# One written order for the transfers of two queues, a written buffer layout, and a new order of all steps, in clustered attention followed by an MLP

## The chip, the cores and the metric

The kernel runs on one core of a Trainium2 chip. The core has TensorE for matrix products (PE in the profile), VectorE (DVE), ScalarE (ACT), GpSimd (POOL) and a sync engine (SP); the last does no arithmetic here and only issues transfers. ACT issues transfers too, between its own computations. The metric is the device time of one execution in microseconds (us).

## The reference: what is computed

Four batches of eight heads, 768 positions, head size 64, all in float32. Each query and each key is put into one of 16 clusters of its head, the one whose normalised centroid it is nearest to. Attention runs only between positions of the same cluster. The heads' outputs, laid side by side, are the input x (4 x 768 x 512) of a second block: a mix over positions by two thin matrices U and V of rank 32, then an MLP of width 2,048 with a residual.

```python
mask = q_assign[:, :, :, None] == k_assign[:, :, None, :]
scores = np.where(mask, scale * np.matmul(q, k.transpose(0, 1, 3, 2)), -1e9)
attn = softmax(scores)                     # over the keys
x = heads_side_by_side(np.matmul(attn, v))
u = x + (x.transpose(0, 2, 1) @ U @ V).transpose(0, 2, 1)
out = u + np.maximum(u @ w_ch1, 0.0) @ w_ch2
```

The second block's weights come as float64 and are turned into float32 on the chip.

## The kernel before, in words

**The work and its order.** `list_work` lists all the work as steps: a call of a small function, or one piece of such a call. `sequence` (line 93) is a list of 4,334 step numbers, the order in which the steps are written out. There is no other schedule: `keep_order` (line 311) ties each instruction to the one written before it on the same engine, so that each engine's own order is the written one. `kept` (line 42) says, with one character for each use, which of a few buffers of a kind each use gets (the probabilities `pr` have 11, the score tiles `st` 2, the general tiles `w` of the matrix results 4, and so on); `place` (line 343) reads it.

**Attention.** It is done in 16 pairs of heads; i is the number of the pair (4 to a batch). Queries and keys are loaded (`load`, R), split into a high and a low part that matmuls take at a faster rate (`split_hi`, `split_lo`), and laid into `arena` (three sets, used in turn) by transfers within the chip: `place_keys_hi`, `place_keys_lo`, `place_queries`, `place_clusters`, and `place_ones`, which fills a row with ones. The one-hot cluster numbers are further rows, scaled so that two positions of different clusters get a score of almost minus infinity. `rowmax` makes the scores once to take each query's maximum on DVE; `rowmax_place` turns the 12 columns of maxima with a matmul, negates them on ACT (mT) and issues a transfer from ACT's queue that lays them into the arena as the row that meets the ones. `scores` makes the scores again, transposed and with the maximum taken off (L781, and L783 which reads the ones and the maxima); ACT takes the exponential (pr, L787); `values` multiplies by v (L805); `weights` adds up the probabilities on POOL, in a few cases on DVE (T, L797). `sums`, `sums_T`, `copy_values` (L811) and `normalise` finish a pair into x (`xt`).

**The mix and the MLP.** `mix_u`, `mix_sum`, `mix_v` do the rank-32 mix; the result goes to memory (u_scr). `fetch_blocks` (line 992) reads it back in eight transfers of 32-row blocks for one half of a batch, and `turn_blocks` transposes the blocks on DVE (L1004). `split_u` makes the high part on ACT (L1016) and the low part on DVE (L1018). The two weight products of the MLP are done by a scheme of seven products of half-size blocks instead of eight: `product` (L1068 to L1070, combined on DVE in L1078 or copied by ACT in L1082), `relu` (L1110 low half on DVE, L1112 high half on ACT), `gemm2` (L1269 to L1271, the second product of batches 0 and 1), and for batches 2 and 3 `product2` (L1215 to L1217), fed by `split_h` (ACT L1142, DVE L1140) and ended by `combine2` and `output`, which sends blocks out in four transfers a time (L1259).

**The weights.** `convert` loads float64 words, joins them to float32 (`join_late`) and stores them to memory (w_scr); `fetch_w` reads one back (w2f, rw). `split_w` and `split_w2` make high and low parts (ACT L1043 and L1052). `sums_w2` reads w_scr with ACT's queue (late_g, turned), adds blocks on POOL and stores the sums from ACT's queue; `keep_w2` and `keep_sums` store from ACT's queue too. `stage_w` reads weights back for batches 2 and 3 (rw, sums_w), `split_staged` splits them (L1164 on ACT, L1162 on DVE or POOL), `load_w2` reads parts for `product2`.

**Transfers.** There are 767: 645 on SP's queue and 122 on ACT's. All those of attention are SP's but one kind, the maxima of `rowmax_place`. A transfer signals its end on a semaphore, of which there are few, so that many transfers share one in turn. In the kernel before only the order on each queue is tied to the written one; how transfers of the two queues follow each other in the turns is left to the framework.

**Buffers.** Tiles of attention lie in pools (`sb` on the left, `late` on the right) that are closed when the MLP opens its own (`open_mlp`, `open_late`); a tile of the MLP that lies over an attention tile waits for that tile's last use. Where a tile lies within its pool follows from when it is first used.

Of the kernel before, what the change touches and what calls it, by code (L numbers as in the profile page):

```python
# [10 lines left out]
F32 = mybir.dt.float32  # L11
F32R = mybir.dt.float32r
# [11 lines left out]
DM = H * D  # L24
# [17 lines left out]
kept = {  # L42
    "R":
        "0101010101010101010110101110100110",
    "rw_g":
        "010110101010101010101010101010101010101010101010101010101010101101001011010101010",
    "rw":
        "0110101010101010101010101010101010010101010110101010",
    "rw_t":
        "0100101010101010110011010101010010101010101010101011001011010011001101001011010",  # L50
    "w":
        "01202301323210210301202012012033022112032101320231303123123212310212310230213013203112010323012013201203213121"
        "02301302301230231011323023101021031212301302321030213023121021023130201320132013201321203103123013021013032102"
        "13021321032012031021012310310231320203121032032102210321030232310312013302320123101232310320120121023310210320"
        "12301320103213010320132102313021301322132013210321020130121320132012301231023132010212013030123023103213032102"
        "31023012313210301230212103312012320123013201023021310321032123021130210203230123012312001302130210303012021013"
        "22012301301032103132012101021302210",
    "pr":
        "0123456789a0123456789a0123456789a0123456789a0123456789a0123465789a132546078a91234560789a1234560789a1234560789a"
        "1234560789a1234560789a12345607891a243560789a12346507891a234506879a123456071892435a60",  # L60
# [5 lines left out]
        "0101010101010101",  # L66
    "mT":
        "01010101010101010",
    "vt":
        "0120121021210210",  # L70
    "st":
        "01010010101010101010101010101010101010101010101010101010101010101010101011001011001010101010101010101010101010"
        "1010101010101010101010101010100110100110101010101010101010101010010110101010010101100101",
# [3 lines left out]
        "01200120120120120120120120120120",  # L77
    "rv":
        "0101010101010101",
    "hh":  # L80
# [3 lines left out]
    "v":  # L84
        "01010101010100110011010101101100111000110101000101010010110101011010001010101010110010101010101010101101010101"
        "100101011011010101100",
    "y":
        "01234540215350342152301540342513124035204153105204123543204130545210352410352134053021352401345202314010532543"
        "51503210421234015343204532015024351023405",
# [1410 lines left out]
```

## Time and profile before

| | |
|---|---|
| time of the runs, us | 967.59, 970.29, 973.48 (median 970.29) |
| the profiled execution, us | 971.04 |
| its span from first to last instruction, us | 969.2 |
| mean granted clock of TensorE | 0.987 |
| busy us: TensorE, its weight loads, DVE, ACT, POOL | 934.8, 747.3, 767.0, 461.9, 642.1 |
| busy share of TensorE | 96% |

In the profile's rows a line such as L783 is a line of the kernel; names are those of tiles, as out<-in. "A <- B C" in a list of waits says that A's engine sat idle until B's instruction that writes C ended; three numbers behind it are the sum in us, how many times, and the longest. SPq and ACTq are the engines' queues of transfers. The granted clock is a share of TensorE's full speed. The chain of waits goes back from the last instruction, at each step to what released it.

### The profile page before, as it was taken

The page shows a single profiled execution, that of the slowest core. Times are in us where ns is not written, and L with a number is a line of the kernel's source. Part 1 is how long each engine was busy: PE and PEld are TensorE (multiplying, and loading weights), DVE is VectorE, ACT ScalarE, POOL GpSimd, SP SyncE. Part 2 cuts the span into 40 slices and gives each one's busy share as a digit, 9 for nine tenths or more (in the row PEclk, how much of TensorE's full clock was granted, in tenths as well). Part 3 has the DMA queues.
Part 4 walks back from the last instruction along what each step waited for, and adds up shares of the span by engine and source line. Part 5 has one row for each costly group of instructions (what it writes and reads, how often), then busy time and mean ns, then how long its engine had stood idle before and what let it go on. Part 6 is the DMA issues. An engine that isn't in the chain of part 4 may idle for free.

```text
span 969.2 us, 14666 instructions
## 1 busy us (share of the span) xinstructions
PE 934.8 (96%) x5098; PEld 747.3 (77%) x5098; DVE 767.0 (79%) x1251; ACT 461.9 (48%) x680; POOL 642.1 (66%) x433
## 2 busy tenths in 40 slices
PE   7999999999999999988899999999899999989997
PEld 5666666666666656644788888889789999989997
DVE  5989988878888877766787768877678988778775
ACT  6545555555555554643433434343434554255440
POOL 6388676788688869985889976875453663137420
PEclk8999999999999999989899999999999999999999
DMA  7666547555756668612548886579768788876686
GB/s 189 177 148 178 143 128 232 141 145 140 212 154 177 179 130 197 74 48 87 196 152 297 313 312 193 160 254 294 209 231 185 166 280 259 227 174 119 231 264 160
DMA packets 169646, 183.13 MB, mean 189 GB/s; under 512 B 110427, under 2 KB 119253, under 8 KB 168549
## 3 DMA queue, kind: packets, MB, share of 16 engines
q1 hardware_dynamic: 136672, 156.21, 58.2%
q10 hardware_dynamic: 32900, 25.99, 8.5%
q8 instruction: 40, 0.66, 0.3%
q14 instruction: 34, 0.27, 0.1%
HBM read 112.72 MB, written 41.42 MB: 159 GB/s over the span
## 4 chain that ended last, share of the span: by engine, by line
PE 82%; DVE 7%; DMA 5%; issue 2%; ACT 2%; POOL 2%; SPq 0%; ACTq 0%; DVEq 0%; POOLq 0%
PE o_ps L805 13%; PE ps_max L750 7%; PE ps_h L1068 7%; PE ps_h L1070 7%; PE ps_h L1069 7%; PE st L781 7%; PE st L783 6%; PE z L1216 4%; PE z L1215 4%; PE z L1217 4%; PE y L1271 4%; PE y L1270 3%; PE y L1269 3%; DVE m L755 2%; PE ps_sum L820 1%
## 5 line engine op out<-in xcount | busy, mean ns | idle before, releaser
L797 POOL TENSOR_TENSOR T<-T,pr 128x768 f32<-128x768 f32 x120 | 223.6, 1867 | 46.2 <-DVE T L797 22.9
L755 DVE TENSOR_REDUCE m<-ps_max 128x1 f32<-128x384 f32 x372 | 189.2, 549 | 45.2 <-PE ps_max L750 43.0
L787 ACT ACTIVATE pr<-st 128x768 f32<-128x768 f32 x186 | 147.2, 811 | 79.9 <-PE st L783 73.3
L805 PE MATMUL o_ps<-pr,vt 128*64 128x384 f32 x768 | 138.8, 499 | 0.0
L1068 PE MATMUL ps_h<-arena,combos 128*128 128x384 f32 x352 | 120.8, 343 | 8.2 <-ACT rw_g L1082 3.5
L1070 PE MATMUL ps_h<-arena,combos 128*128 128x384 f32 x352 | 119.3, 339 | 0.0
L1069 PE MATMUL ps_h<-arena,combos 128*128 128x384 f32 x352 | 119.2, 339 | 0.0
L750 PE MATMUL ps_max<-arena 128*128 128x384 f32 x372 | 113.0, 368 | 2.4 <-DVE m L755 1.6
L805 PEld LDWEIGHTS o_ps<-pr,vt 128*64 128x64 f32 x768 | 50.3, 138 | 65.2 <-issue 60.0
L781 PE MATMUL st<-arena 128*128 128x384 f32 x372 | 100.1, 350 | 0.4 <-ACT pr L787 0.4
L783 PE MATMUL st<-arena 97*128 97x384 f32 x372 | 96.3, 340 | 2.9 <-DMA arena<-ones 2.4
L750 PEld LDWEIGHTS ps_max<-arena 128*128 128x128 f32 x372 | 65.8, 188 | 42.0 <-DVE m L755 18.1
L797 POOL TENSOR_TENSOR T<-pr 128x768 f32<-128x768 f32 x30 | 56.1, 1870 | 53.8 <-ACT pr L787 49.5
L781 PEld LDWEIGHTS st<-arena 128*128 128x128 f32 x372 | 65.0, 189 | 18.4 <-issue 9.0
L1068 PEld LDWEIGHTS ps_h<-arena,combos 128*128 128x128 f32 x352 | 66.9, 190 | 15.3 <-DVE c L1078 5.3
L1271 PE MATMUL y<-w,hl 128*128 128x512 f32 x192 | 76.3, 397 | 1.3 <-DVE hl L1110 1.3
L1270 PE MATMUL y<-w,hh 128*128 128x512 f32 x192 | 76.0, 396 | 0.0
L1269 PE MATMUL y<-w,hh 128*128 128x512 f32 x192 | 75.2, 392 | 0.0
L1162 POOL TENSOR_TENSOR combos<-rw,combos 128x1024 fp32r<-128x1024 f32 x10 | 24.0, 2402 | 74.3 <-ACT combos L1164 74.3
L783 PEld LDWEIGHTS st<-arena 97*128 97x128 f32 x372 | 68.4, 190 | 3.5 <-issue 2.7
L1069 PEld LDWEIGHTS ps_h<-arena,combos 128*128 128x128 f32 x352 | 67.0, 190 | 2.3 <-issue 0.2
L1070 PEld LDWEIGHTS ps_h<-arena,combos 128*128 128x128 f32 x352 | 66.9, 190 | 0.0
(213 smaller groups left out, 2078.8 us busy)
## 6 DMA issues: line engine op xcount, KB each, us to landing
combos<-w_scr SPq DMA_DIRECT2D x112, 256.0 KB
R<-in_qk SPq DMA_DIRECT2D x32, 384.0 KB
arena<-arena SPq DMA_DIRECT2D x64, 192.0 KB
arena<-arena SPq DMA_DIRECT2D x31, 384.0 KB
late_rw<-in_w SPq DMA_DIRECT2D x20, 512.0 KB
u<-u_scr SPq DMA_DIRECT2D x96, 96.0 KB
rw<-w_scr SPq DMA_DIRECT2D x15, 512.0 KB
vt<-in_v SPq DMA_DIRECT2D x16, 384.0 KB
```

The lines of the kernel that those rows point to most:

```text
L750: nc.tensor.matmul(ps[:, 0:HS], x1[:, 0, g // 2, g % 2, t * P:(t + 1) * P], x1[:, 1, h, g % 2, :], start=True, stop=True)
L755: nc.vector.reduce_max(live["m2", i][:, h, u:u + 1], ps[:, 0:HS], axis=AX.X)
L781: nc.tensor.matmul(st[:, j, 0:HS], x1[:, 1, hk, j, ks], x1[:, 0, h, j, :], start=True, stop=False)
L783: nc.tensor.matmul(st[:, j, 0:HS], x2[0:97, 1, hk, j, ks], x2[0:97, 0, h, j, :], start=False, stop=True)
L787: nc.scalar.activation(pr, st[:, :, 0:HS], AF.Exp, scale=SCALE)
L797: eng.tensor_add(T, live["p", i, h, 0] if c == 1 else T, live["p", i, h, c])
L805: nc.tensor.matmul(o_ps[64 * j:64 * j + 64, 0:HS], vv[:, c, j, :], pr[:, j, :], start=(c == 0), stop=(c == NT - 1))
L1068: nc.tensor.matmul(ps, ah[:, d], oh[:, d], start=(d == 0), stop=False)
L1069: nc.tensor.matmul(ps, ah[:, d], ol[:, d], start=False, stop=False)
L1070: nc.tensor.matmul(ps, al[:, d], oh[:, d], start=False, stop=(d == 1))
L1270: nc.tensor.matmul(y, hh[:, f, ts], w2[:, 1, f, :], start=False, stop=False)
L1271: nc.tensor.matmul(y, hl[:, f, ts], w2[:, 0, f, :], start=False, stop=(g in lasts and f == 1))
```

## The change

Three things are changed, and no step, no instruction and no engine of a step.

`keep_order` ties a transfer not only to the instruction before it on its engine but also to the transfer written before it on either queue:

```diff
-def keep_order(tc, first=0):
+def keep_order(tc):
 
     last = {}
-    for ins in tc.nc.cur_bb.bb.instructions[first:]:
-        if ins.engine in last:
-            tc.add_manual_dep(ins, last[ins.engine], mybir.DependencyInfo(
+    for ins in tc.nc.cur_bb.bb.instructions:
+        lines = (ins.engine, "transfers") if isinstance(ins, mybir.InstDMACopy) else (ins.engine,)
+        for name in dict.fromkeys(last[line] for line in lines if line in last):
+            tc.add_manual_dep(ins, name, mybir.DependencyInfo(
                 mybir.DependencyClass.NoSync, mybir.DependencyReason.DATA), reason="program order")
-        last[ins.engine] = ins.name
+        for line in lines:
+            last[line] = ins.name
```

These ties make no instruction wait; they only fix the order in which the framework goes through them when it gives out semaphores.

The tiles of attention (and of the pool with the MLP's hidden halves) get their places in the order of a written list, by one tile made for each name when the pool is opened:

```diff
+    def beds(home, **columns):
+
+        for tag, n in columns.items():
+            home.tile([P, n], F32, name="bed", tag=tag, bufs=1)
+
+    beds(sb, scale0=32, scale1=32, mx0=24, mx1=24, m0=12, m1=12, m20=24, m21=24, mT0=128, mT1=128,
+         sims=HS, oh=HS, ohT=HS, **{f"vt{k}": 2 * HS for k in range(3)}, **{f"pr{k}": 2 * HS for k in "0123456789a"})
+    beds(late, T0=2 * HS, T1=2 * HS, rep=96, v3=S, xt=4 * S, x3=DM, xu=DM, os0=HS, os1=HS, os2=HS, T2=2 * HS, sums=HS,
+         u_w=NT * RK, rv0=12, rv1=12, sel=32)
...
         live["w2", 0] = mx.tile([P, 2, 2, 512], F32R, name="w2_0")
+        beds(mx, w2f=1024, hh0=2 * HS, hl0=2 * HS, hh1=2 * HS, hl1=2 * HS, hh2=2 * HS, hl2=2 * HS)
...
-        live["late_w"] = (right.tile([P, 2, 512], I64, name="late_rw"), right.tile([P, 2, 512], F32, name="late_g"),
-                          right.tile([P, 512], F32, name="joined"))
+        raw_w = right.tile([P, 2, 512], I64, name="late_rw")
         live["w2f"] = right.tile([P, 1024], F32, name="w2f_odd")
+        live["late_w"] = raw_w, right.tile([P, 2, 512], F32, name="late_g"), right.tile([P, 512], F32, name="joined")
```

The tiles that had no such name before (sims, oh, ohT, sums, xt, x3, xu, u_w, v3, rep, sel, scale, w2f) get one. `sequence` and `kept` are written anew. `sequence` holds the same 4,334 numbers in another order; its first and last line, as an example (most of the other lines differ too):

```diff
 sequence = [
-    1, 0, 2, 6, 110, 107, 3, 108, 16, 12, 13, 14, 4, 40, 7, 109, 5, 11, 17, 9, 15, 8, 10, 18, 24, 117, 111, 25, 19, 20, 21,
...
+    4326, 4320, 4327, 4323, 4328, 4329, 4330, 4331, 4332, 4333, 2317, 2329, 2389, 2401, 2413, 2425]
```

Half of the steps stand at most 4 places from where they stood; one in twenty stands 14 or more places earlier, one in twenty 15 or more later. Read out of the two lists, by their places (step: place in `sequence`, from 0; transfer: place among the 767 transfers as written):

| | before | after |
|---|---|---|
| transfer of the maxima of pair 15 (`rowmax_place`) | step 2245, transfer 369 | step 2245, transfer 369 |
| `place_ones(15)` | step 2211, transfer 366 | step 2170, transfer 358 |
| `fetch_blocks(1, 1)`, eight transfers | step 2181, transfers 358 to 365 | step 2177, transfers 360 to 367 |
| `fetch_blocks(2, 1)`, first reading | step 3198, transfers 487 to 494 | step 3186, transfers 486 to 493 |
| `sums_w2(6, 7)` and `sums_w2(7, 0)` | steps 3209, 3212, transfers 495, 496 | steps 3209, 3208, transfers 496, 495 |
| the eight transfers ahead of `fetch_blocks(2, 1)` | steps 3145 to 3197 | steps 3143 to 3177 |
| `stage_w(27, 0)` | step 3854, transfer 645 | step 3858, transfer 649 |
| `output(2, 6, 0)`, four transfers | step 3856, transfers 646 to 649 | step 3848, transfers 645 to 648 |
| `output(3, 1, 1)`, four transfers | step 4207, transfers 713 to 716 | step 4243, transfers 723 to 726 |
| `output(3, 1, 0)`, four transfers | step 4240, transfers 725 to 728 | step 4261, transfers 732 to 735 |
| `split_h(4, 3)` high, `split_h(5, 1)` high, `split_h(5, 2)` high | steps 4247, 4249, 4256 | steps 4248, 4252, 4260 |
| `relu(0, 0)` low | step 2394 | step 2405 |
| the additions of `mix_v(3, ...)` on DVE | steps 2388 to 2407 | steps 2389 to 2403 |
| `gemm2(0, 1)` | step 2420 | step 2417 |
| `convert(13, 3)`, a store | step 2555 | step 2498 |
| `fetch_w(0, 1)`, second reading | step 2575 | step 2551 |
| `split_w2(0)` high, second | step 2593 | step 2603 |

## Rows read from the trace of the kernel before

**Rows 1.** page, busy time, share of the span and instructions of each engine
```profile
PE 934.8 (96%) x5098; PEld 747.3 (77%) x5098; DVE 767.0 (79%) x1251; ACT 461.9 (48%) x680; POOL 642.1 (66%) x433
```

**Rows 2.** waits of PE, whole run: sum us, times, longest us
```profile
PE ps_h L1068 <- ACT rw_g L1082: 3.5, 2, 2.6
PE ps_h L1068 <- DVE c L1078: 3.3, 4, 2.5
PE st L783 <- DMA arena<-ones: 2.4, 1, 2.4
...
PE ps_h L881 <- DVE xt L883: 2.0, 2, 1.2
...
PE y L1271 <- DVE hl L1110: 1.3, 1, 1.3
...
PE z L1216 <- DVE combos L1140: 0.6, 1, 0.6
...
PE z L1215 <- ACT combos L1142: 0.2, 1, 0.2
```

**Rows 3.** windows: length, busy of PE PEld DVE ACT POOL, granted clock, DMA share, GB/s
```profile
418.50:425.00 6.50, 6.47 (x19) 3.26 (x20) 3.37 (x3) 1.51 (x2) 6.50 (x3) 0.51 0.35 132
701.30:704.70 3.40, 3.40 (x11) 3.21 (x11) 2.78 (x3) 1.19 (x2) 3.32 (x3) 0.50 0.84 328
856.50:860.00 3.50, 3.50 (x21) 3.50 (x21) 2.59 (x6) 2.88 (x5) 1.32 (x1) 1.00 0.91 135
```

**Rows 4.** chain of waits, 410 to 420 us: start, length, what
```profile
413.21 1.91 DMA arena<-mT
...
415.14 0.30 SPq L998
...
416.06 2.33 DMA arena<-ones
...
418.52 0.98 PE st L783 x2
```

**Rows 5.** waits of SP's queue, whole run: sum us, times, longest us
```profile
SPq L429 <- DMA arena<-mT: 28.0, 7, 6.5
...
SPq L998 <- DMA arena<-mT: 21.1, 3, 11.9
...
SPq L998 <- DMA w_scr<-late_rw: 5.1, 1, 5.1
```

**Rows 6.** chain of waits, 684 to 701 us
```profile
686.55 7.05 DMA late_g<-w_scr
...
693.62 3.80 DMA u<-u_scr
...
700.34 0.44 PE ps_h L1068
```

**Rows 7.** chain of waits, 846 to 858 us
```profile
846.97 3.46 DMA sums_w<-w_scr
...
850.45 0.32 ACTq L1259
...
850.82 2.38 DMA out_y<-u
...
856.40 0.44 PE ps_h L1068
```

**Rows 8.** chain of waits, 936 to 969 us
```profile
938.30 3.78 DMA out_y<-u
942.10 0.32 ACTq L1259
```

**Rows 9.** chain of waits, 455 to 470 us
```profile
463.58 1.37 DVE hl L1110
```

**Rows 10.** chain of waits, 505 to 524 us
```profile
510.05 7.20 DMA w_scr<-w2f
...
517.27 3.97 DMA w2f<-w_scr
```

More of the change, by code (lines that the diff above doesn't have):

```diff
@@ L42 @@
 kept = {
-    "R":
[L44 to L50, printed above, removed]
-    "w":
[L52 to L57, printed above, removed]
+    "rw_g":
+        "010110101001101010101010101010101010101010101010101010101010101101001011010101010",
@@ new lines @@
+    "rw":
+        "0101010101010101010101010101010101011010101001101001",
+    "rw_t":
+        "0100101010101010110011010101010010101010101010101010110011001010110100101011010",
+    "R":
+        "0101010101010101010101101101100110",
+    "w":
+        "01023201123320303102303203032301103120230122303312101231231231233032003121213021301202312032030123012301321232"
+        "01031203102130231021213023102023012323101023103213201032312030231102312030123021023132130201213012020312031203"
+        "21031203213023012230102320123120310310322103013203320132013102031123012103213031203212301320213030231012320130"
+        "21302310210210301230231203121032102133201312302123030120320123201323012310231203230123021021303102101321032102"
+        "31203113021310203213022301231023103123021302031032121032013230132120320133210321302010310320130102102030223330"
+        "12302110221201030210232032021303320",
@@ L58 @@
     "pr":
-        "0123456789a0123456789a0123456789a0123456789a0123456789a0123465789a132546078a91234560789a1234560789a1234560789a"
-        "1234560789a1234560789a12345607891a243560789a12346507891a234506879a123456071892435a60",
+        "0123456789a1023456789a10234567891a023456789a1023456789a0123456789a032456178a9024356178a90234561789a0234561789a"
+        "2034561789a0234561789a02435617890a235461789a0234651789a02354167890a2354617809234a561",
     "mx":
@@ L66 @@
         "0101010101010101",
+    "vt":
+        "0120121021201210",
     "mT":
         "01010101010101010",
-    "vt":
-        "0120121021210210",
     "st":
-        "01010010101010101010101010101010101010101010101010101010101010101010101011001011001010101010101010101010101010"
-        "1010101010101010101010101010100110100110101010101010101010101010010110101010010101100101",
+        "01010100101010101010101010101001101010101001101010101010101010101010101010101011001010101001101010101010110010"
+        "1010101010101010110010101010010110100110101010101010100110101010011011010010101100101010",
     "T":
@@ L76 @@
     "os":
-        "01200120120120120120120120120120",
+        "01200120120120120120120120120210",
     "rv":
         "0101010101010101",
+    "v":
+        "01010101010101010011010101110100110101010101001001010101010101010110010100110010101010101010101010101101010100"
+        "101101011100101101010",
     "hh":
@@ L83 @@
         "01210210210212021021021021021201",
-    "v":
-        "01010101010100110011010101101100111000110101000101010010110101011010001010101010110010101010101010101101010101"
-        "100101011011010101100",
-    "y":
-        "01234540215350342152301540342513124035204153105204123543204130545210352410352134053021352401345202314010532543"
-        "51503210421234015343204532015024351023405",
+    "y":
+        "01234505421304231541032542130542313045120451013254032054135243254010342510342135044352013212530430215041340523"
+        "14032410125425013032534523140025341023504",
 }
 sequence = [
[207 rows of a table removed]
[207 rows of a table added]
 def pieces(n):
@@ L439, in clustered_attention_moe @@
     obi = one.tile([P, 1], F32, name="obi")
-    sel = late.tile([P, 32], F32, name="sel")
-    rep = late.tile([P, 96], F32, name="rep")
+    sel = late.tile([P, 32], F32, name="sel", tag="sel", bufs=1)
+    rep = late.tile([P, 96], F32, name="rep", tag="rep", bufs=1)
     onehot = [one.tile([P, NT, 4, 32], BF16, name="oh_0")]
@@ L458, in constants @@
                 nc.gpsimd.memset(x[64:96, 1].rearrange("p h j q -> p (h j q)").bitcast(F32), 0.0)
-            parts["scales"] = [sb.tile([P, 32], F32, name=f"scale{k}") for k in range(2)]
+            parts["scales"] = [sb.tile([P, 32], F32, name=f"scale{k}", tag=f"scale{k}", bufs=1) for k in range(2)]
             for t, (q, k) in zip(parts["scales"], ((1.0, BIG), (0.0, -BIG))):
@@ L514, in norms @@
         nc.vector.reciprocal(rn, n1)
-    u_w = late.tile([P, NT, RK], F32, name="u_w")
-    v3 = late.tile([96, S], F32R, name="v3")
+    u_w = late.tile([P, NT, RK], F32, name="u_w", tag="u_w", bufs=1)
+    v3 = late.tile([96, S], F32R, name="v3", tag="v3", bufs=1)
     def load_mix(k, stage):
@@ L568, in sims @@
         yield
-        sm = live["sims", i] = sb.tile([P, HS], F32, name="sims", bufs=1)
+        sm = live["sims", i] = sb.tile([P, HS], F32, name="sims", tag="sims", bufs=1)
         nc.scalar.mul(sm, ps[:, 0:HS], c_rn[:, i % NP:i % NP + 1])
@@ L626, in clusters @@
         yield
-        live["oh", i] = sb.tile([P, HS], F32, name="oh", bufs=1)
+        live["oh", i] = sb.tile([P, HS], F32, name="oh", tag="oh", bufs=1)
         nc.vector.transpose(live["oh", i], live.pop(("flat", i)))
@@ L634, in clusters_T @@
     def clusters_T(i):
-        live["ohT", i] = sb.tile([P, HS], F32R, name="ohT", bufs=1)
+        live["ohT", i] = sb.tile([P, HS], F32R, name="ohT", tag="ohT", bufs=1)
         nc.scalar.activation(live["ohT", i], live.pop(("oh", i)), AF.Identity, scale=scales[0][:, 0:1], bias=scales[1][:, 0:1])
@@ L821, in sums @@
         yield
-        live["sums", i] = late.tile([P, HS], F32, name="sums")
+        live["sums", i] = late.tile([P, HS], F32, name="sums", tag="sums", bufs=1)
         nc.scalar.copy(live["sums", i], ps[:, 0:HS])
@@ L845, in normalise @@
         if ("x", b) not in live:
-            live["x", b] = late.tile([P, NT, DM], F32, name="xt")
+            live["x", b] = late.tile([P, NT, DM], F32, name="xt", tag="xt", bufs=1)
         nc.vector.tensor_tensor(
@@ L862, in mix_u @@
         yield
-        live["xu", b] = late.tile([P, DM], F32, name="xu")
+        live["xu", b] = late.tile([P, DM], F32, name="xu", tag="xu", bufs=1)
         nc.scalar.copy(live["xu", b], ps)
@@ L870, in mix_sum @@
         yield
-        x3 = live["x3", b] = late.tile([96, DM], F32R, name="x3")
+        x3 = live["x3", b] = late.tile([96, DM], F32R, name="x3", tag="x3", bufs=1)
         nc.scalar.copy(x3, ps[0:96, :])
@@ L939, in weight_tile @@
             return place(raw, "rw", [P, 512], I64, "rw").bitcast(F32)
-        return live["w2f"] if k % 2 else pool["mx"].tile([P, 1024], F32, name="w2f")
+        return live["w2f"] if k % 2 else pool["mx"].tile([P, 1024], F32, name="w2f", tag="w2f", bufs=1)
     homes = {m: turned[:, k] for k, m in enumerate(("b11", "b12", "b21", "b22", "t3"))}
```

412 rows, old and new, of the table sequence are left out of this document.

## The prediction

> **What bounds the kernel now.** I read the page first: TensorE is busy 934.8 of 969.2 us [rows 1], so no other engine can be the bound and a new order can win only what TensorE loses. That is two things: time in which it has nothing to do (969.2 - 934.8 = 34.4 us), and time at half speed. So the second view is the list of what TensorE waited for [rows 2]: the reader is to see that it is short and that a handful of single waits of 0.9 to 2.6 us carry most of it. The third is the table of stretches [rows 3]: behind the wait at 416 us TensorE ran 6.5 us at a granted clock of 0.51, behind the one at 698 us 3.4 us at 0.50, but behind the one at 854 us at 1.00. These are the two levels of 1.2 and 2.4 GHz; at half speed half of the stretch is lost. Only then did I follow the chain back from each large wait [rows 4, 6 to 10], and of the six that I followed five end in a transfer.
>
> The case at 416 us is the clearest. The matmul of L783 started at 418.52, when the ones row landed (issued 416.06, 2.33 us). The ones row stood on SP's queue behind a read of u_scr (L998), and that read was let go at 415.14, when the copy of the row maxima, issued on ACT's queue at 413.21, had landed [rows 4]. The read shares no data with that copy, and in the written order it is transfer 364 and the copy 369. So the read waited for a transfer that is written behind it: the two must share a semaphore, given out in an order that is not the written one. SP lost 11.9 us there, 21.1 us in three such waits at L998 and 28.0 us in seven at L429 [rows 5]. Counted along both queues, the pairs that wait on each other fit a rotation of eight semaphores: a transfer waits for the one eight turns ahead of it. Eight is my estimate from these pairs.
>
> **The change part by part.** No instruction is added or removed: the same 4,334 steps, the same tiles, the same engine for each. Three things move.
>
> *One order for the transfers of both queues.* Turns on the semaphores now follow the written order, so a transfer can be held only by one written eight ahead of it. Each held case, with its new turn:
>
> (a) 416 us. The ones row moves from transfer 366 to 358, ahead of the second group of reads; the copy of the maxima stays at 369, and the first transfer it can hold is 377. Both the hold and the queue in front of the ones row go. Next in line is the copy of the maxima itself: it landed at 413.21 + 1.91 = 415.12, and TensorE came to L783 at 418.52 - 2.4 = 416.1 [rows 2, 4], so it is hidden with 1 us to spare. The reads that the ones row passes go out behind its issue, but without the hold, so earlier than before. Gain 2.4 us. If the half-speed stretch goes too, 6.5 x 0.49 = 3.2 us [rows 3].
>
> (b) 698 us. The eight reads of batch 2's second half (L998) were held on SP until a copy on ACT's queue, issued at 686.55, had landed 7.05 us later; the last read was issued at 693.62 and landed 3.80 us after, and DVE's transposes, ACT's split and ACT's copy of a product followed, until the matmul at 700.34 [rows 6]. That copy belongs to step sums_w2(7,0), written after the reads in both orders. In the new one the reads are transfers 486 to 493 and follow one another; the transfers they can be held by (478 to 485) are written 9 steps and more ahead. TensorE's wait is 2.6 us, the longest of its group [rows 2]. The reads need come only that much earlier, and the hold alone was 5.1 us, booked to ACT's store just ahead of that copy [rows 5]. Gain 2.6 us, and 3.4 x 0.50 = 1.7 us of clock [rows 3].
>
> (c) 854 us. ACT stood in its own output copies: one waited for a weight read of SP's (846.97, 3.46 us), the next was issued and ACT came free at 853.2; its split, DVE's split and two combinations followed, until the matmul at 856.40 [rows 7]. In the new order that weight read, stage_w(27,0), stands behind the four output copies (transfer 649, they 645 to 648), so it can't hold them. But the 2.38 us between the next copy and ACT's next work is the copies' own issue, beside SP's reads, and need not shrink. Bounds 0 and 2.5 us, the longest of its group [rows 2]; I take 1.5, nearer the upper end, since the hold that goes (850.45 - 846.97) is longer than the wait.
>
> (d) 943 us. The same on ACT: four output copies, the last let go 3.78 us after the first, then split_h, DVE, and a matmul [rows 8]. The group of output(3,1,0) moves behind the three splits it stood ahead of (step 4240 to 4261), but that of output(3,1,1) moves close ahead of them (4207 to 4243), now four turns in a row. TensorE waited 0.6 us on DVE and 0.2 on ACT there [rows 2]; I take 0.8, bounds -1.3 (the new group's four issues of 0.32 us [rows 8], with nothing to hide them) and 0.8.
>
> *Moved steps without a hold.* (e) At 464 us the low half of relu(0,0) stood on DVE between two additions of the rank mix and cost the chain 1.37 us [rows 9]; it now comes behind all six additions, and its reader, gemm2(0,1), behind one more product, which hides it (1.4 us if not). TensorE's two waits there sum to 2.0 us [rows 2]. I take 1.4. (f) At 522 us ACT waited for a weight read that had waited for a store of 7.20 us [rows 10]; the store moves 57 steps earlier, the read 24. TensorE's wait is the other of its group, 3.5 - 2.6 = 0.9 us [rows 2]; I take it whole: 57 steps are 12.7 us at the mean pace of 4,334 steps in 969 us. (g) At 568 us a low half on DVE follows ACT's high half directly; the order around it is not plainly better, so the 1.3 us [rows 2] stay.
>
> *The written layout of attention's buffers.* It adds no instruction and costs nothing by itself; what it can do is make an MLP tile wait for another attention tile. The first of them is combos1, which now lies over the first buffers of attention, among them the value tile of pair 15. Its first writer stands on ACT behind the copy of pair 15's output, which waits for the same matmuls, so I take 0. Rows of such a wait there are none; I bound it by no more than the 2.6 us of the largest wait [rows 2] either way.
>
> Sum: gaps 2.4 + 2.6 + 1.5 + 0.8 + 1.4 + 0.9 = 9.6 us; clock 3.2 + 1.7 = 4.9 us; together 14.5. The profiled execution took 971.04 us (span 969.2 and 1.8 around it), 0.75 above the median of the runs. 971.0 - 14.5 - 0.7 = **956 us**.
>
> The clock is the term I trust least. The rows show two falls behind waits of 2.4 and 2.6 us and none behind one of 2.5 us [rows 2, 3]. The Trainium skill (TensorE: Matmul & The Clock Gate, What's actually happening) says that the clock is gated by how busy the engine has recently been; by that rule alone both half-speed stretches go with their waits, which is the sum above. By the row at 854 us the fall is not tied to the wait, and without the 4.9 us the sum would be 961. I stay with the rule here, since both falls have their wait just ahead.
>
> **The rivals.**
> - *Nothing comes of it* (966 to 973). The waits that go uncover the next one: at 416 us the hidden copy of the maxima has 1 us of cover, at 698 us DVE's transposes and two ACT steps remain in the chain [rows 6]. Or the change doesn't do what it says: the edges order the instructions, but the turns are still given otherwise; then only (e) and (f) act, 970.3 - 2.3 = 968. For it: of the 34.4 us of idle [rows 1] most is in waits that the order shares out anew. Against: three of the four largest waits have the hold as their root. The Trainium skill (DMA: Bandwidth & Descriptors, Issuing engines are not separate DMA queues) speaks for this rival: it says that a second issuing engine saves only issue time, usually small, so the order between two queues should matter little. By that rule (a) to (d) are worth a few issues of 0.3 us [rows 4, 8], and the time would be about 967; the 11.9 us hold [rows 5] disagrees.
> - *Slower: the output copies hold ACT and SP in turn* (975 to 980). Between 818 and 858 us the new order puts five weight reads (stage_w) and batch 3's reads each eight turns behind an output copy, and output copies eight behind weight loads. An ACT copy that waits stops ACT's computing. Where the planned instants are off, each hold lasts one landing, 2.4 to 3.8 us [rows 7, 8]; five of them in series are 15 us, which eat the gain, and each may bring 1.7 to 3.2 us of half speed: 956 + 15 + 2 x 3 = 977. It decides once a hold outlasts the matmuls queued, as in (c). Against it: most such pairs are written ten steps or more apart.
> - *More than the sum* (940 to 950). If the new order also takes a third of the idle I did not touch, (34.4 - 9.6) / 3 = 8 us, 956 - 8 = 948. For it: all waits in the list are single ones [rows 2]; against: nothing in the order around (g) shows it.
>
> **How the numbers follow.** Forecast (951 to 964) 0.54, more than the sum 0.17, nothing 0.19, slower 0.10. Half a percent, 4.9 us, is what a measurement tells from no change; below 965.4 all of the first two cases lie: faster 0.71, same 0.19, slower 0.10. The range reaches to the middle of the third and fourth case: 944 to 969.
>
> **What would show it.** Right: no wait of SP's L998 on the copy of the maxima, and the 2.4 us wait on the ones row, the 2.6 us one on ACT's rw_g and the 0.5 clock around 418 and 701 us gone; TensorE busy about 930 us in a span near 955. Wrong: SP still waiting for transfers written behind; ACT idle behind output copies between 835 and 860 us; or the same idle of TensorE behind other steps.

## The result and the profile after

| | before | after | ratio, 95% interval |
|---|---|---|---|
| median of the runs, us | 969.16 | 957.37 | 0.9876 (0.9836 to 0.9915) |
| profiled execution's span, us | 969.2 | 955.6 | |
| the kernel after again, beside other runs on another chip, us | 971.17 | 959.93 | 0.9882 (0.9859 to 0.9906) |

The forecast was 956 and faster; it is 957.4, and faster beyond the interval. By the medians the gain is 11.8 us; the two profiled executions, which are taken apart below, differ by 13.6 us. The page of the kernel after gives TensorE 7.5 us less busy time than [rows 1] and 6.1 us less idle time (34.4 before, 28.3 now):

```profile
PE 927.3 (97%) x5098; PEld 743.7 (78%) x5098; DVE 757.1 (79%) x1251; ACT 461.0 (48%) x680; POOL 653.4 (68%) x433
```

What TensorE waited for over the whole run (sum, times, longest). Lines of the kernel after stand 12 to 13 further down than those of before:

```profile
PE ps_h L1081 <- DVE rw_t L1091: 4.9, 1, 4.9
...
PE ps_h L1081 <- DVE c L1091: 1.2, 3, 0.6
PE ps_h L1081 <- DVE xt L859: 1.2, 1, 1.2
...
PE y L1284 <- DVE hl L1123: 0.7, 1, 0.7
```

Of the waits in [rows 2], those of L783 on the ones row, of L1068 on rw_g and the 2.5 us one on c are gone. New are the longest of either list, 4.9 us on rw_t (from 519.0 to 523.9 us), and one of 2.5 us on a load at the very start (rw_g<-in_c; 0.5 us before). The stretches show the clock (length, busy time of the engines, granted clock, DMA share, GB/s), first three that answer to [rows 3], then one at half speed that begins inside the new wait and ends 4.1 us behind it:

```profile
414.00:420.00 6.00, 6.00 (x34) 3.94 (x33) 4.91 (x3) 4.05 (x7) 5.92 (x4) 1.00 0.00 1
690.00:700.00 10.00, 10.00 (x53) 9.04 (x52) 4.72 (x7) 5.53 (x8) 9.84 (x6) 1.00 0.44 171
846.00:856.00 10.00, 10.00 (x59) 10.00 (x59) 8.04 (x17) 5.97 (x10) 3.18 (x2) 1.00 0.89 196
521.20:528.00 6.80, 4.01 (x11) 3.63 (x12) 5.10 (x10) 0.85 (x1) 4.02 (x5) 0.50 0.66 226
```

SP's waits for transfers at the line of the reads (L1011, before L998) are small, and no wait of SP on the maxima (arena<-mT) is left at any line; before they were 28.0 us at L429 and 21.1 at L998 [rows 5]:

```profile
SPq L1011 <- DMA out_y<-u: 3.5, 4, 1.6
SPq L1011 <- DMA u<-u_scr: 2.6, 1, 2.6
```

**How the turns go.** The semaphore events in the traces show the mechanism. Each transfer signals on one of eight semaphores, and both queues use the same eight. In the kernel after, and in every kernel below with the tie, a transfer has the semaphore of the one written eight places ahead of it in all 759 cases that there are; in the kernel before in 380 of 759. Before, SP waited eight times, 29.2 us in all, for a transfer written behind the waiting one; with the tie it never does. So the estimate of eight holds, and the change does what it says. One reading of the prediction needs a correction. Two of the three waits of reads on the maxima at L998 (11.9 and 6.0 us) were on a copy written behind, the third (3.2 us) on the one just ahead. But of the seven at L429 (28.0 us) all but one of 0.7 us were on a copy written just ahead, which had the same semaphore one turn away instead of eight.

**Where the 13.6 us lie.** Both kernels run the same 5,098 matrix instructions in different orders. I gave each matrix instruction the median time from its start to the next one's start, taken over all of its kind in the two traces compared, added these up in either order, and read at which moment each kernel had done the same amount of work. The table gives the gain on the kernel before by stretch (in its times, us), one profiled execution for each kernel. The control, the kernel after again, differs from the kernel after by up to 1.9 us in a stretch: less than that is read only together with a wait in the trace. The first two columns share what falls at their border and can shift against each other by up to 0.8 us. A row is a single execution and its sum is not the difference of the medians: that of the new order not tied is the fastest of its 11 (968.55, median 971.18), that of the store first the fastest of its 4 (949.09, median 950.58).

| stretch | 0-400 | 400-440 | 440-520 | 520-545 | 545-690 | 690-840 | 840-870 | 870-end | sum |
|---|---|---|---|---|---|---|---|---|---|
| forecast | 0 | (a) 5.6 | (e) 1.4 | (f) 0.9 | (g) 0 | (b) 4.3 | (c) 1.5 | (d) 0.8 | 14.5 |
| after | 4.7 | 6.0 | 1.1 | -6.0 | 0.7 | 4.1 | 2.1 | 1.0 | 13.6 |
| after again (control) | 5.4 | 5.5 | 2.4 | -7.5 | -1.2 | 2.7 | 2.6 | 0.8 | 10.6 |
| new order, not tied | 3.9 | 6.1 | 1.6 | -5.8 | -6.5 | 0.3 | 2.4 | 0.7 | 2.7 |
| old order, tied | -3.1 | 5.6 | -0.7 | -0.7 | -0.3 | 0.9 | 2.7 | 1.3 | 5.8 |
| old order, ones row early | -1.1 | 5.6 | 0.3 | 0.4 | -0.1 | -0.3 | -1.0 | 0.5 | 4.3 |
| old order, tied, stage_w moved | -4.8 | 5.6 | -0.2 | 0.8 | -4.6 | 3.7 | 1.9 | 0.4 | 2.9 |
| after, store first | 5.1 | 6.0 | 2.1 | 0.9 | 0.1 | 4.1 | 2.6 | 1.1 | 21.9 |

### The profile page after: what moved, and what is told of

It is laid out like the page before. It is cut to its first block, busy times and chain, and to the rows that moved or that the text cites. A ratio compares the mean times of both kernels' runs of the same rounds, so it can differ in the third digit from the quotient of the medians.

```text
span 955.6 us, 14706 instructions
## 1 busy us (share of the span) xinstructions
PE 927.3 (97%) x5098; PEld 743.7 (78%) x5098; DVE 757.1 (79%) x1251; ACT 461.0 (48%) x680; POOL 653.4 (68%) x433
## 4 chain that ended last, share of the span: by engine, by line
PE 76%; DVE 9%; DMA 7%; issue 3%; POOL 2%; ACT 2%; SPq 1%; ACTq 0%; DVEq 0%; POOLq 0%
PE o_ps L817 11%; PE ps_max L762 7%; PE ps_h L1081 7%; PE ps_h L1083 7%; PE ps_h L1082 7%; PE st L793 6%; PE st L795 6%; PE z L1228 4%; PE z L1229 4%; PE z L1230 4%; PE y L1284 3%; PE y L1283 3%; PE y L1282 3%; DMA arena<-arena 2%; PE ps_sim L578 1%
## 5 line engine op out<-in xcount | busy, mean ns | idle before, releaser
L809 POOL TENSOR_TENSOR T<-T,pr 128x768 f32<-128x768 f32 x120 | 226.3, 1890 | 36.1 <-DVE T L809 18.3
L817 PE MATMUL o_ps<-pr,vt 128*64 128x384 f32 x768 | 136.2, 493 | 0.0
L1081 PEld LDWEIGHTS ps_h<-arena,combos 128*128 128x128 f32 x352 | 66.6, 189 | 10.1 <-DVE c L1091 3.5
```

The lines of the kernel that those rows point to most:

```text
L809: eng.tensor_add(T, live["p", i, h, 0] if c == 1 else T, live["p", i, h, c])
L817: nc.tensor.matmul(o_ps[64 * j:64 * j + 64, 0:HS], vv[:, c, j, :], pr[:, j, :], start=(c == 0), stop=(c == NT - 1))
L1081: nc.tensor.matmul(ps, ah[:, d], oh[:, d], start=(d == 0), stop=False)
```

## The experiments

The runs came in three groups, each on one chip with the kernel before beside it; the ratios are to that kernel (medians 969.34, 972.24 and 971.17 us).

### Order or tie: four runs

**old_order_tied** takes only the new `keep_order`, as it stands in the section on the change; `sequence`, `kept` and layout stay.

> The kernel before with one edit: the transfers of both queues tied into their written order. Sequence, buffers and layout stay as before. Theory A (the tie carries the three large holds at 416, 698 and 854 us): their waits of 2.4, 2.6 and 2.5 us and both half-speed stretches behind the first two go, so 969 falls by some 6.0 + 3.6 + 2.1 = 11 to 12 us, to 957 to 960; the mix at 460 us, the 1.3 us wait on hl at 568 us and the attention part up to 400 us stay as they were. Theory B (the new order of the steps carries the gain, and the tie is only bookkeeping): 966 to 972, with the wait on the ones row near 416 us still there. In between (962 to 965): the tie removes the holds, but this order, which was not written for it, gets new ones elsewhere.

Measured: 965.17, ratio 0.9956 (0.9943 to 0.9970). In between, just above the third case (962 to 965). At 416 and 854 us both waits are gone (5.6 and 2.7 us in the table). At 697 us 2.2 of the 2.6 us are still there. These are TensorE's waits between 660 and 720 us, SP's longest between 676 and 702 us, and the last read's piece of the chain (start, time to landing); lines stand 2 further down than before:

```profile
PE ps_h L1070 <- ACT rw_g L1084: 2.2, 1, 2.2
PE ps_h L1070 <- DVE c L1080: 1.1, 1, 1.1
```

```profile
SPq L1157 <- DVE combos L1043: 10.1, 1, 10.1
```

```profile
686.68 10.38 DMA u<-u_scr
```

The reads are no longer held by a transfer. They stand on SP's queue behind stage_w(17, 0) (L1157), which waited 10.1 us for a buffer that DVE still read; before, the same step waited 8.3 us there. So the first read went out at 681.75, hardly before the 682.53 of the kernel before. Without the hold the last one followed at 686.68, 6.9 us earlier than before (693.62), but it landed at 697.06, and before at 697.42: it took 10.38 us instead of 3.80 [rows 6]. ACT's stores and copies, issued from 685.8 to 690.3, now ran beside it. The first 60 us got 2.4 us longer, with a wait of 0.9 us on the first copy of the maxima at 37.9 us and half speed from 37.0 to 43.8. A likely reason, not tried singly: before, SP stood 3.8 us for that copy, which landed in 4.24 us; with the tie SP sends two more transfers into the arena and a load beside it, and it took 5.08 us.

**new_order_untied** is the other half: everything new but the tie.

```diff
-def keep_order(tc):
+def keep_order(tc, first=0):
...
-    for ins in tc.nc.cur_bb.bb.instructions:
-        lines = (ins.engine, "transfers") if isinstance(ins, mybir.InstDMACopy) else (ins.engine,)
...
+    for ins in tc.nc.cur_bb.bb.instructions[first:]:
+        if ins.engine in last:
...
```

> The kernel after with one edit: transfers are again tied only to their own queue. The new order of the steps and the written layout stay. Theory A (the tie carries the holds): reads of u_scr and transfers into the arena are again held by copies of ACT's queue that are written behind them, SP's waits at those lines rise from 0 to 10 us and more, and the time rises from 957 to 962 to 970, by single waits of TensorE of 2 to 3 us with half speed behind them. Theory B (the order carries the gain): 955 to 959, no such waits. The 4.9 us wait near 518 us (a store queued behind loads on SP) has nothing to do with the tie and stays under both.

Measured: 971.18, ratio 1.0028 (1.0015 to 1.0040): theory A, a little beyond its range. Without the tie the new order wins nothing. The holds are back: SP waits nine times, 53.7 us in all, for transfers written behind. These are its longest groups over the whole run, TensorE's waits that are new between 640 and 720 us, and the wait of DVE that links them (lines 2 above those of after):

```profile
SPq L1009 <- DMA arena<-mT: 24.0, 3, 12.9
SPq L1009 <- DMA late_g<-w_scr: 14.4, 2, 10.5
```

```profile
PE ps_h L1079 <- DVE rw_t L1089: 4.4, 1, 4.4
PE y L1282 <- DVE hl L1121: 2.6, 2, 1.9
```

```profile
DVE turned L1015 <- DMA u<-u_scr: 7.6, 2, 5.4
```

Reads were held 3.9 us until 665.37 and 10.5 us until 690.55, each by a copy into late_g written behind them, and DVE's transposes waited for those reads.

The table puts the whole difference of the two profiled executions, 10.9 us, behind 545 us (14.7 us by the ratios). Up to 400 us this kernel keeps 3.9 of the 4.7 us, at 416 us all 6.0: those belong to the order.

**ones_early** is the kernel before with one step moved.

```diff
 (steps as written)
+place_ones(15)
 fetch_blocks(1, 1)
 ... 29 steps ...
-place_ones(15)
```

> The kernel before with one step moved: place_ones(15) stands 30 places earlier, ahead of fetch_blocks(1, 1) on SP's queue. Nothing is tied. Theory A (at 416 us TensorE pays for the queue in front of the ones row, and the half speed follows from that wait): the 2.4 us wait goes and with it the 6.8 us at half speed, so the stretch 400 to 440 us is 5 to 6 us shorter and the time 963 to 965, even where the reads of u_scr are still held by the copy of the maxima. Rival 1 (the clock has its own reason): 2.4 us gained, half speed still there, 966 to 967. Rival 2 (the reads' hold moves to another transfer that the scores need): no gain, 968 to 971.

Measured: 965.56, ratio 0.9952 (0.9931 to 0.9973); the gain at 400 to 440 us is 5.6, theory A by its place; the time is 0.6 above its range. The hold is still there, and TensorE does not feel it (SP's wait between 395 and 425 us, at L1020, which is L998 before; then the stretch 412 to 418 us):

```profile
SPq L1020 <- DMA arena<-mT: 12.4, 1, 12.4
```

```profile
412.00:418.00 6.00, 5.75 (x32) 3.52 (x32) 4.14 (x6) 2.52 (x5) 6.00 (x4) 1.00 0.15 25
```

So at 416 us the move alone and the tie alone each give the whole gain, and together they give it once.

**tied_stage** is old_order_tied with one step moved.

```diff
 (steps as written)
-stage_w(17, 0)
 ... 4 steps ...
 fetch_blocks(2, 1)
+stage_w(17, 0)
```

> The kernel before with the tie and one moved step: stage_w(17, 0) stands behind fetch_blocks(2, 1) instead of five places ahead of it. It is to be read against the kernel before with the tie alone (965.2), where TensorE still waited 2.35 us at 697 us. Theory A (that wait is left because SP stood 10.1 us in stage_w(17, 0), waiting for DVE's combos, with the eight reads queued behind it): the reads are issued some 8 us earlier, the wait falls below 0.8 us, the 1.2 us one at 692 us may go with it; 961 to 963.5. Rival (the last read took 10.4 us to land among other transfers, and would land late wherever it stands): the wait stays above 1.5 us, 964 to 966.

Measured: 965.94, ratio 0.9932 (0.9910 to 0.9955), against 0.9956 for the tie alone: 2.3 us by the ratios, with intervals that overlap. At its place the 2.2 us wait is gone, and this is the only wait of TensorE from 660 to 720 us (L1092 is L1070 with the tie alone):

```profile
PE ps_h L1092 <- DVE c L1102: 0.5, 1, 0.5
```

By the table 690 to 840 us gains 3.7, where the tie alone had 0.9. The sum does not show it, since this execution had a 3.0 us wait at 615 us behind a weight read that took 7.5 us, and a 2.6 us wait at 37 us; neither was there in the run with the tie alone at that size. The run leaves the cause in part argued. Because this execution came about 4 us later to the place, its first read went out at 681.36, only 0.4 us earlier by the clock, not 8; against the work around it, it is some 4 us earlier. The reads landed by 689.3, before ACT's transfers, which went out from 689.28. So what helped is that the reads were ahead both of stage_w's wait and of ACT's transfers; the run does not part the two, nor does it rule out the late execution itself.

### The lost 6 us at 520 us: two runs

The chain of waits of the kernel after, 503 to 524 us (start, length, what), shows what TensorE waited for:

```profile
503.31 2.78 DVE joined L399
...
506.14 0.33 SPq L928
...
507.04 6.25 DMA w_scr<-w2f_odd
...
513.72 8.63 DMA w_scr<-joined
...
522.44 0.06 DVE joined L394
...
523.47 0.47 DVE rw_t L1091
523.94 0.04 issue
523.99 0.69 PE ps_h L1081
```

Read it from the end: the matmul waits for DVE's rw_t, which stands on DVE behind a rewrite of the buffer `joined`; that waits for the store of the old `joined`; the store stands on SP behind a read (L1037) of the weight that the store of w2f_odd writes; and that store stands behind a load (L928) that waits for DVE's step ending at 506.09 (503.31 + 2.78). **store_first** moves the store ahead of the load:

```diff
 (transfers of SP as written)
+convert(15, 3)      store of w2f_odd
 convert(18, 0)      load, waits for DVE
 convert(17, 0)      load
-convert(15, 3)
```

> The kernel after with one step moved: the store convert(15, 3) stands five places earlier, ahead of the loads convert(18, 0) and convert(17, 0) on SP's queue. Theory A (the store was ready at about 495 us but queued behind a load that waits for a DVE step ending at 506 us; so the read of that weight, the next store and then DVE, which rewrites the next store's source, came late one after the other): the 4.9 us wait of TensorE near 518 us goes or falls under 1 us, and the 6.8 us at half speed behind it go too; gain 4.9 + 3.4 = 8 us at most, 950 to 953 after what waits next. Rival (DVE waits because the store of the joined half itself takes 8.6 us to land among other transfers): the store lands as late as before, the wait stays at 3 us or more, 956 to 959.

Measured: 950.58, ratio 0.9811 (0.9794 to 0.9828), in the range of theory A: 6.3 us by the ratios, of 8 at most. SP's transfers in the kernel after and then here (start, length of issue; lines of kernels with moved steps stand 23 below those of after):

```profile
506.14 0.81 SPq L928 DMA_DIRECT2D late_rw<-in_w  x2
507.04 0.38 SPq L935 DMA_DIRECT2D w_scr<-w2f_odd  x1
513.35 0.33 SPq L1037 DMA_DIRECT2D w2f_odd<-w_scr  x1
513.72 1.32 SPq L932 DMA_DIRECT2D w_scr<-joined  x1
```

```profile
497.06 0.32 SPq L958 DMA_DIRECT2D w_scr<-w2f_odd  x1
504.73 0.81 SPq L951 DMA_DIRECT2D late_rw<-in_w  x2
505.77 0.33 SPq L1060 DMA_DIRECT2D w2f_odd<-w_scr  x1
506.14 0.43 SPq L955 DMA_DIRECT2D w_scr<-joined  x1
```

The store is issued 10 us earlier and the next one 7.6 us earlier. TensorE has no wait there, and the clock stays full:

```profile
515.00:525.00 10.00, 10.00 (x50) 8.90 (x50) 8.52 (x15) 2.24 (x3) 9.33 (x8) 1.00 1.03 387
```

**loads_in_turn** does the same and also puts convert(17, 0) ahead of convert(18, 0).

```diff
 (transfers of SP as written)
 convert(15, 3)
+convert(17, 0)
 convert(18, 0)
-convert(17, 0)
```

> The kernel after with the store convert(15, 3) ahead of both loads, as in the run at 950.6, and the load convert(17, 0), whose buffer is free some 10 us earlier, ahead of convert(18, 0). Theory A (what is late after the store is no longer a load): 6 to 8 us faster than the control, the same as with the store alone within 1 us. Theory B (the earlier load lets ACT and DVE join the next weight earlier): 7 to 9 us faster, with DVE's idle around 500 to 540 us shorter. Rival (the gain of that run came from its chip or its execution): under 4 us.

Measured: 952.83, ratio 0.9808 (0.9786 to 0.9831), on the chip on which the control has 959.93 (0.9882): 7.1 us faster, theory A. The second move adds nothing: SP now issues the first of the two loads at 497.75 and stands 8.2 us before the second, 7.4 of them in a wait for DVE.

### The written layout: three runs

**new_order_no_beds** is the kernel after without the tiles made ahead.

```diff
     def beds(home, **columns):
-        for tag, n in columns.items():
-            home.tile([P, n], F32, name="bed", tag=tag, bufs=1)
+        pass
```

> The kernel after with the written layout taken out: no tile is made ahead, so each attention buffer lies where its first use puts it; order and ties stay. Theory (the layout is worth nothing by itself): 956 to 959, no new wait of TensorE above 1 us. Rival (it keeps MLP tiles off attention buffers that are still in use): a wait of 1 to 3 us appears between 430 and 480 us, where the first MLP tiles are written over attention's, and the time is 959 to 962.

Measured: 963.33, ratio 0.9907 (0.9880 to 0.9933). The table's method puts 2.1 us of loss at 450 to 475 us, with waits of 1.3 and 0.6 us at the products there: the rival. It was run again with the kernel after beside it, as **after_again** and **no_beds_again**:

> The kernel after, unchanged, beside the two that follow, on one chip: a control. A ratio of 0.986 to 0.990 to the kernel before; the 4.9 us wait of TensorE near 518 us and no wait above 1 us at product(1, 2) near 463 us if these belong to the kernel, another list of waits if they belong to one execution.

> The kernel after without the written layout, a second time, beside the control. Theory (without it the tile operands lies over xt, and ACT's split waits for the store of xt to memory, so the waits of 1.5 and 0.8 us near 463 and 468 us come again): 1.5 to 3 us slower than the control, with that wait of ACT of about 9 us again. Rival (the store landed late by chance): the wait of ACT is under 5 us and the two times agree within 1 us.

Measured: 959.93 (0.9882, 0.9859 to 0.9906) for the control, 962.78 (0.9916, 0.9897 to 0.9935) without the layout, 2.9 us slower. The intervals just overlap, but both pairs of runs agree (0.9876 and 0.9907, 0.9882 and 0.9916). The wait came again on ACT, here between 435 and 475 us, and with it TensorE's, here from 430 to 540 us. In the first row of these the 5.3 us are the wait near 520 us, which the control has too; the other 0.7 and the 1.7 us lie near 465 us:

```profile
ACT operands L1028 <- DMA u_scr<-xt: 9.6, 1, 9.6
```

```profile
PE ps_h L1080 <- DVE rw_t L1090: 6.0, 2, 5.3
PE ps_h L1080 <- ACT rw_g L1094: 1.7, 1, 1.7
```

The control has no wait of ACT on that store. Without the list, the MLP's tile `operands` lies over xt, as this wait shows, and ACT's split waits until xt has landed in memory. The trace of the kernel before has no such wait either: what the layout does is keep the new order from this one. The old order with the layout was not run.

### The mix, and a sum of small moves: two runs

**relu_between** puts the low half of relu(0, 0) back between two additions of the mix, in the kernel after.

```diff
 (steps of DVE as written)
 mix_v(3, 2)
+relu(0, 0) low
 mix_v(3, 3)
 mix_v(3, 4)
 mix_v(3, 5)
-relu(0, 0) low
```

> The kernel after with one step moved back: the low half of relu(0, 0) on DVE stands between two additions of the rank mix again, ahead of the fourth. Theory (the additions are the chain there, so its 0.96 to 1.37 us goes onto it): TensorE's stretch from 440 to 470 us is 0.9 to 1.4 us longer, 958 to 959.5. Rival (the next step is late anyway, by ACT's split or the weights): within 0.3 us of the kernel after in that stretch.

Measured: 960.77, ratio 0.9886 (0.9857 to 0.9914), by its time no different from the kernel after. Its place shows between the theory and the rival: TensorE waited 1.2 us for the additions there (first row), in the control 0.4 (second), so the low half costs 0.8 us.

```profile
PE ps_h L916 <- DVE xt L918: 1.2, 3, 0.8
```

```profile
PE ps_h L893 <- DVE xt L895: 0.4, 2, 0.2
```

**best** is loads_in_turn with six more moves:

```diff
 (steps as written)
-join_late(31) second, join_late(30) first
 product(10, 6) combination
+join_late(31) second, join_late(30) first
...
-split_w(0) high, low
 relu(15, 1) high, low
+split_w(0) high, low      each behind its half of relu
...
+normalise(14, 0)
 weights(15, 0, 5)
...
-turn_blocks(1, 1, 1)
 normalise(14, 1)
+turn_blocks(1, 1, 1)
-normalise(14, 0)
```

> The kernel after with the store moved as in the run at 950.6, and with it seven more small moves: the load convert(17, 0) ahead of convert(18, 0), whose wait it does not share; two joins of weights (join_late) on DVE behind the combination that product(11, 0) waits for; the high and low half of split_w(0) behind those of relu(15, 1); two of normalise(14) ahead of a sum and of a transpose on DVE. Each is meant to take away a single wait of TensorE of 0.8, 0.8 and 0.6 us. Theory (such waits are worth their own length): 947.5 to 949.5. Rival (as with the store, a moved step makes another late): 950 to 954.

Measured: 952.93, ratio 0.9804 (0.9773 to 0.9835), the same as with the store alone: the rival. One wait shrank (0.7 to 0.2 us at gemm2(15, 5)), one stayed (product(11, 0), 0.6 us), and three are new: 0.9 us at product(16, 3), 0.4 at gemm2(9, 2), and this one at 438.6 us, where normalise was moved, with 3.4 us at half speed behind it:

```profile
PE ps_sum L855 <- ACT rw_g L1118: 2.2, 1, 2.2
```

So the version to keep is the kernel after with the store ahead of its load, 1.9% under the kernel before.

## Why the prediction was right, and where it was not

The time, the direction and the main places were right, and what was to show it right came: no wait of SP on the maxima, the waits at 416 and 697 us and the half speed behind them gone, TensorE busy 927 us where I said about 930. Of what was to show it wrong, two signs came in part: ACT idle behind output copies between 835 and 860 us, and a new idle stretch of TensorE behind another step, the 4.9 us. That the total came within 1.4 us of the forecast is luck: two errors of opposite sign, +4.7 us up to 400 us and -6.9 us at (f), largely cancel.

**(a) 416 us: right in size, half right in cause.** 6.0 us for 5.6, wait and half-speed stretch together. I gave the gain to the tie and the move at once; the runs show that either is enough, and that the hold itself costs TensorE nothing once the ones row stands ahead of the reads.

**(b) 697 us: right in size (4.1 for 4.3, in the control 2.7), wrong in cause.** The step that failed reads: "The reads need come only that much earlier, and the hold alone was 5.1 us". It takes the reads to be earlier by the hold, and their 3.80 us to landing to stay as they are. With the hold gone and nothing else changed the last went out 6.9 us earlier and landed at almost the same moment, 10.38 us after its issue, beside ACT's transfers; the first went out only 0.8 us earlier, since stage_w(17, 0) stood ahead of it on SP. The new order moves that step from 3193 to 3228, behind the reads; in the kernel after all eight go out from 672.8 to 676.8, before ACT's next copy at 678.3. I followed the reads past the transfers that hold them by a semaphore, but not past those that stand ahead of them on SP, and did not ask what would travel beside them. The other way round the tie is needed as well: the new order without it loses 10.9 us against the kernel after here and just before.

**(c), (d) 854 and 943 us: right.** 2.1 and 1.0 us for 1.5 and 0.8; TensorE's waits at both places are gone, and the differences are smaller than what two executions of one kernel show. At 854 us again the order without the tie has the gain (2.4), and so does the tie without the order (2.7).

**(e) the mix: right in kind.** The low half costs 0.8 us between the additions, not 1.4; the stretch that held (e) gained 1.1.

**(f) 522 us: wrong, and the largest error.** "I take it whole" was argued from the 57 places by which convert(13, 3) moves. Its wait did go; but in the same stretch convert(15, 3) moves from 2559 to 2584, behind two loads, and that made a chain of four transfers and buffers end at TensorE 4.9 us late. Of the 6.8 us at half speed around it TensorE was busy for 4.0, half of which is lost: 4.9 + 2.0 = 6.9 us, the whole step from the +0.9 that I forecast to -6.0. It is the mechanism of the rival "slower" at another place: a transfer that waits with others queued behind it. I looked for it at the output copies between 818 and 858 us. There ACT was held, 5.7 us behind output copies (before 16.7) and 5.5 us behind a weight load, as its waits between 822 and 862 us show, but TensorE waited only 0.2 us:

```profile
ACT combos L1177 <- DMA out_y<-u: 5.7, 2, 3.8
ACT combos L1177 <- DMA combos<-w_scr: 5.5, 1, 5.5
```

**The part up to 400 us: 4.7 us that I did not forecast,** 3.9 of them without the tie. It is the rival "more than the sum" in kind: many small waits on DVE, such as the 0.8 us at 96 us, are shared out anew. A half-speed stretch of 6.8 us at 11.8 us of before is gone too, though the first 30 us are only 0.5 us shorter. Which moves do it was not tried singly.

**The layout:** neither trace has such a wait, as taken, but left out of the new order it costs 2.9 us, just over the 2.6 that I gave as its bound. The tile that then waits is operands, not combos1, which I named as the first to look at.

**The rival "nothing", and the clock.** The new order tied and not tied differs by 0.0152 of the time of before, 14.7 us, so the order between the two queues is worth far more than a few issues of 0.3 us. The Trainium skill (DMA: Bandwidth & Descriptors, Issuing engines are not separate DMA queues) says that issuing from several engines saves only the time of the issue. No run here changes which engine issues, so this stays untested; what the runs refute is what I inferred from it, that the order between two queues should matter little. Both half-speed stretches that I counted in went with their waits (1.00 at 414 to 420 and 690 to 700 us). The Trainium skill (TensorE: Matmul & The Clock Gate, What's actually happening) says that the clock follows how busy the engine has been of late; the trace agrees at these two places, and the last section shows waits that alone do not tell whether the clock falls.

## What to carry to other kernels

When the order of work is written by hand, the order in which transfers of several queues get their semaphores has to be written too: an order that was planned for it is worth nothing without it (1.0028), and it is worth less than half as much to an order that was not (0.9956). Follow every moved transfer past what stands ahead of it on its own queue, ask what each of these waits for, and what will travel beside it once a hold is gone; a store behind a load that waits for a buffer put the stretch around it 6.0 us behind, as much as the largest single place won (6.0 us at 416 us). Once the list of TensorE's waits past the start holds only single waits of about a microsecond, moving steps shifts them more than it removes them (0.9811 and 0.9804).

## What the runs showed that I had not expected

Half speed does not follow from the length of a wait alone. Past 30 us, every wait of TensorE of 2.4 us or more had a stretch at 0.5 around its end or just behind it, in all runs and with one exception, the 2.5 us at 854 us of the kernel before [rows 3]. But one of 1.9 us at the same place in ones_early had it, and one of 2.2 us at 697 us in old_order_tied had not (first and second row; the second holds the whole wait, 697.8 to 700.0):

```profile
852.00:855.40 3.40, 3.40 (x12) 3.40 (x12) 2.91 (x6) 2.74 (x4) 0.41 (x1) 0.50 0.89 170
```

```profile
697.50:703.00 5.50, 3.31 (x18) 2.89 (x17) 4.18 (x8) 3.42 (x5) 5.09 (x3) 1.00 0.39 131
```

The stretch around the mix (440 to 475 us), with several short waits of 1.3 us at most in most runs, ran part of its way at half speed in every run. And one kernel does not repeat its small waits: in the control the wait at 518 us was 6.6 us instead of 4.9, and waits of 0.9 and 1.3 us stood at 630 and 696 us that the first execution had not in that size.
